# Chunk attention and a hypermixer token MLP on one core: units of 512 tokens by four heads, loads held in line by GpSimd, stores on two queues

## The chip, the core and the metric

The kernel runs on one NeuronCore of a Trainium2 chip. Its engines have a queue of instructions each: PE (TensorE, matmuls; its weight loads are PEld), DVE (VectorE), ACT (ScalarE), POOL (GpSimd) and SP (SyncE, which here only issues DMAs). An engine runs its own queue in order and waits for the others by semaphores. Sixteen DMA engines move data between HBM and the on-chip memory SBUF; matmuls write into PSUM, which has eight banks of 2 KB per partition. The metric is the time of one execution in microseconds on the device, the median of several; all durations below are microseconds.

## The reference

```python
# q, k, v: (8, 8, 576, 64) float32: batch, heads, tokens, head_dim
q_c, k_c, v_c = (x.reshape(B, H, 9, 64, D) for x in (q, k, v))   # chunks of 64 tokens
scores = np.matmul(q_c, k_c.transpose(0, 1, 2, 4, 3)) / np.sqrt(D)
scores = scores - np.max(scores, axis=-1, keepdims=True)
attn = np.exp(scores)
attn = attn / (np.sum(attn, axis=-1, keepdims=True) + 1e-09)
x = np.matmul(attn, v_c).reshape(B, H, S, D).transpose(0, 2, 1, 3).reshape(B, S, H * D)
wq, wk = x @ w_q, x @ w_k                    # w_q, w_k: (512, 64)
W_tok = np.einsum('bsd,btd->bst', wq, wk) / np.sqrt(64)
mixed = np.einsum('bst,btd->bsd', W_tok, x)
out = np.maximum(mixed, 0.0) @ w_out         # w_out: (512, 512); out: (8, 576, 512) float32
```

Attention stays inside chunks of 64 tokens, nine to a batch. The mixing that follows has no softmax, so the kernel forms G = wk^T x (64 x 512) once per batch and then wq G for each token.

## The kernel before, in words

**Units.** Of the nine chunks of a batch, eight make two whole units of 256 tokens by all eight heads (16 units in all); the ninth chunks of two batches make one rest unit (4). `pairs` lists the 20. A whole unit goes through these steps, each named as below and, by its line, in the profile:

- tq and tk (L365): 16 PE transposes each of q and of k into one PSUM bank. Copies (helper `copy`, L287) bring them to SBUF: k in one piece (`kt`, 128x512), q in two halves of 64 partitions into `qbd`, a block-diagonal tile whose other places hold zeros.
- S (L389): 16 matmuls of 128x64, scores of two heads at a time through the block-diagonal q.
- mx and sub on DVE (L402, L412), exp on ACT (L422), E (L434): 8 transposes of the exponentials, and a copy `et`.
- V twice (L464): 16 quarter matmuls each (64x64 of the array, 65 columns, the last a column of ones for the sum), then den, rec and x on DVE (L477, L481, L491).
- xT (L511) and its copy `xt`; pj (L521), both projections in one; `wt`; wkT (L538) and `wk`.

When all of a batch has come so far: G (L575) and its copies `g`, then for each unit mix (L616), relu `rm` (ACT L631 or DVE L629), out (L643) by 512-column matmuls, and the copy into an `osb` tile. Rest units do the same at half the width (tqr, L349).

**What sets the order.** Nothing is scheduled by rule. The table `ORDER` is a list of words such as `6P0`: step 6, on PE, into PSUM bank 0 (V is DVE, S is ACT). `w7` and `n7` are fillers, matmuls on a tile of ones (L675), 512 and 128 columns wide, 9 and 43 of them. `Graph.write` emits the words one after the other, so each engine's queue has them in that order. Buffers come in rings whose depths stand in `RINGS`; a ring that is full makes the next writer wait.

**Loads.** `LOADS` is the order of the loads, all issued by POOL (`load_qk` L204, `load_v` L212, `load_rest` L219), except the first q and k (`wide`), which SP loads as f32 and DVE and ACT cast. A load of q or k of a unit reads 128 rows x 8 heads in pieces of 512 B (two tokens, R = 2), one of v pieces of 256 B, and casts to f16 on the way. There are seven homes for q and k and a ring of ten units (20 tiles) for v. A load is put in POOL's queue once the step that last read its home stands in the order.

```python
def load_qk(u, t):
    nc.gpsimd.dma_start(qk[u][:, t], rows_of((q, k)[t], u))
```

**Stores.** 56 stores, all on SP: 16 of 128 rows (`i == 0`) and 40 of 64. They are held back until the gate, a one-element DMA (L231) that SP waits with for load 76 (counted from 0), the last; then SP issues those held so far (L234), and afterwards each as its `osb` is ready (L226).

```python
def open_gate(of):
    nc.sync.dma_start(gate[:], of)
    st["open"] = True
    for to, x in held:
        nc.sync.dma_start(to, x)
```

Of the kernel before, what the change touches and what calls it, by code (L numbers as in the profile page):

```python
# [20 lines left out]
5V 4V 0S 1S w7 w7 w7 w7 n7 n7 n7 n7 n7 n7 n7 n7 n7 n7 n7 n7 6P0 2V 3S 7V w7 n7 n7 n7 n7 n7 n7 n7 n7  # L21
9P1 8S n7 n7 34P2 10S 35S 11P0 31P2 12V 32S 13V 33S w7 w7 n7 n7 n7 n7 n7 n7 n7 n7 56P3 36P4 58S 14S
59V 37V n7 n7 n7 91P2 57S 15P0 92S 60P3 38V 94P1 93S 95S 61V 39S w7 n7 n7 n7 n7 n7 96P4 62V 116P1
16S 97V 40P3 63S 21P6 41S 64P0 98V 118S 17P2 65S 18V 22V 99S 66P4 23V 19V 24V 117S 67V 20V 100P0
42P6 68V 46P2 69V 25P1 43V 47V 70P4 44V 26S 45V 101S 48V 71S 49V w5 n5 n5 n5 n5 n5 119P1 102P4 120S
106P2 50P0 107V 108V 27P1 109V 51S 72P6 28S 103V 52P0 73S 74P1 29P6 121P2 53S 75V 54P0 30V 163P1
122V 55S 76P0 164S 160P6 77V 104V 78S 105V 79P0 123V 80S 110P7 85P4 124S 83P0 86V 111S 125P1 84S
81P4 126V 161S 162S 127P0 131P2 112P5 128V 132V 129V 133V 89P6 130V 113S 82S 134V 165P0 90S 114P4
135P2 166V 87P3 136S 137P2 167V 88S 138S 210P5 139P2 295P3 115V 140S 211V 168S 141P0 212V 185P1 213V
142S 298V 214P2 143S 169P4 186S 215V 144P6 170V 188P0 145S 216V 150P4 189S 187V 175P6 146P2 296S  # L30
176V 217S 297V 177V 190P0 178V 147S 380P3 151S 191V 218P2 245P6 219V 247S 299P4 192V 248P5 246S
148P2 249S 300V 193S 152P0 301V 149S 382V 220P6 171P4 153S 194P1 221V 172V 173V 383S 154P2 222V 195S
223V 381S 174V 200P0 155S 196P6 224P3 201V 156P4 202V 197V 225S 203V 179P2 226P3 198V 180S 199V
250P0 302S 181P2 157V 204P6 251V 182S 303P4 205S 158P2 304S 227S 252V 183P5 384P4 184S 206P3 159S
228P5 330P6 207S 229V 208P0 332V 273P1 209S 253S 230P0 385V 358P2 331S 231V 270P3 274V 232S 271S
386V 233P0 359S 272V 305P6 333P4 234S 306V 307V 275P2 308V 334S 239P0 276V 237P5 240S 254P4 277V
238S 335P0 255S 241P5 336V 278S 355P2 242S 256P6 337V 279P3 357S 309P4 280S 243P5 257V 258V 356S
259V 281P0 310S 285P2 244S 260P6 282V 235P4 283V 286V 338S 261V 284V 311P5 262V 287V 360P0 263V 312S
236S 339P5 288V 387S 264P6 361V 289P2 265S 388P3 313P4 290S 266P6 362V 291P2 267S 340S 268P6 415P7
389S 314V 269S 292S 390P0 345P4 293P2 391V 418P3 346V 294S 347V 363S 392V 348V 315P2 443P6 393V 316S  # L40
341P4 419S 394P0 342V 364P1 317S 343V 395V 416S 318P2 344V 396P0 365S 417V 324P4 349P1 325V 350S
444S 397V 366P4 319S 370P0 440P6 367V 368V 371V 509P7 372V 441S 373V 420P2 369V 442S 320P0 421V 511S
351P1 510S 374P4 352V 321S 445P6 422V 375S 326P1 446V 376P0 423S 322P2 327S 377V 424P3 447V 398P0
353P1 378P4 399S 484P5 354S 487P0 379V 323S 425V 400P1 448S 488V 430P2 426P6 485S 328P4 431V 432V
427V 433V 486S 449P0 428V 329V 402S 489P2 401S 429V 403P4 490V 434P1 404S 409P6 450S 491V 556P4 410S
# [17 lines left out]
v19a k15 k14 v12a q14 v11a v11b v12b v19b q15 v18a q17 q18 v14b k18 k17 v15b v17b k16 v17a q19 v15a  # L63
v18b v16a k19 v16b
# [643 lines left out]
```

## Time and profile before

| | us |
|---|---|
| median of 3 runs | 141.2 |
| the runs | 138.96, 141.2, 141.28 |
| profiled execution, span | 138.2 |
| PE busy | 121.3 (88%) |
| DVE busy | 107.2 (78%) |
| ACT busy | 99.9 (72%) |
| POOL busy (loads' issues, mostly) | 70.3 (51%) |
| gate, SP waits for it | 92.7, until 95.5 |
| last matmul ends | 130.84 |

The profiled execution is one of its own beside the three timed ones; the page gives its span, 138.2, and no other time for it. In the rows below, `out<-in` are names of tiles, `x16` counts instructions, `| 15.5, 578 |` is the busy time of a group in us and the mean of one in ns, and what follows is the idle time just before them and what ended it. PEclk is the clock granted to PE, 1.00 being full.

### The profile page before, as it was taken

What the parts mean: (1) busy time and instruction counts of PE and PEld (TensorE: products, weight loads), DVE (VectorE), ACT (ScalarE), POOL (GpSimd) and SP (SyncE); (2) the same over time, 40 slices, a digit from 0 to 9 for tenths busy, and PEclk for the clock granted to TensorE, in tenths of its full rate; (3) what the DMA queues carried; (4) which work ended last, traced back from release to release, by engine and by line L of the source; (5) the groups of instructions that cost most, each with busy time, mean ns of one, the idle gap of its engine ahead of it and who ended that gap; (6) DMA issues with size and microseconds to landing.
All of it is one profiled execution on the core that took longest, in us unless ns stands there. A gap on an engine that the chain in (4) does not pass through costs nothing.

```text
span 138.2 us, 5123 instructions
## 1 busy us (share of the span) xinstructions
PE 121.3 (88%) x2184; PEld 88.0 (64%) x2184; DVE 107.2 (78%) x212; ACT 99.9 (72%) x186; POOL 70.3 (51%) x93
## 2 busy tenths in 40 slices
PE   5839996998999999999999949998999999999800
PEld 2627784785578757777677838677785866645300
DVE  6443699879698999999998969999999989644200
ACT  3333699656868988889998939697999886468400
POOL 8999999965658479587959867200000000000000
PEclk9975799999999999999999999999999999999995
DMA  3999999999999999999999999992788596888895
GB/s 113 228 162 178 164 158 162 187 180 137 143 165 175 150 163 183 174 166 168 173 165 167 177 173 170 165 142 22 197 249 254 155 312 196 283 267 181 235 283 143
DMA packets 86185, 25.11 MB, mean 182 GB/s; under 512 B 78994, under 2 KB 81554, under 8 KB 86162
## 3 DMA queue, kind: packets, MB, share of 16 engines
q0 software_dynamic: 78544, 14.29, 140.4%
q1 hardware_dynamic: 7618, 10.49, 26.3%
q8 instruction: 17, 0.28, 0.8%
q14 instruction: 6, 0.05, 0.1%
HBM read 29.62 MB, written 9.44 MB: 283 GB/s over the span
## 4 chain that ended last, share of the span: by engine, by line
PE 67%; ACT 15%; DVE 5%; DMA 5%; issue 3%; SPq 1%; ACTq 0%
PE ps L643 20%; PE ps L365 9%; PE ps L521 6%; PE ps L389 5%; PE ps L616 5%; PE ps L511 5%; PE ps L434 5%; DMA osb<-in_k_dram 5%; PE ps L464 5%; ACT es L422 4%; PE ps L575 3%; ACT qbd L287 3%; ACT et L287 2%; DVE sh L412 2%; PE ps L675 2%
## 5 line engine op out<-in xcount | busy, mean ns | idle before, releaser
L643 PE MATMUL ps<-wo,rm 128*128 128x512 f16 x144 | 36.2, 379 | 0.3 <-ACT rm L631 0.2
L212 POOL DMA_DIRECT2D v_all<-in_v_dram x32 | 28.4, 894 | 7.9 <-DMA v_all<-in_v_dram 2.0
L402 DVE TENSOR_REDUCE mx<-ps 128x16 f32<-128x1024 f32 (+1 forms) x20 | 22.2, 1111 | 4.6 <-PE ps L389 4.1
L491 DVE TENSOR_TENSOR xs<-ps,rec 128x512 f16<-128x512 f32 x36 | 24.1, 686 | 0.5
L365 PE MATMUL ps<-ident,qk 128*64 128x128 f16 x512 | 21.3, 230 | 3.2 <-DVE qk L287 1.6
L365 PEld LDWEIGHTS <-qk 128*64 128x64 f16 x512 | 16.8, 115 | 6.3 <-ACT qk L287 1.8
L422 ACT ACTIVATE es<-sh 128x1024 f16<-128x1024 f32 (+1 forms) x20 | 19.5, 977 | 1.4 <-DVE sh L412 1.1
L643 PEld LDWEIGHTS <-rm 128*128 128x128 f16 x144 | 12.5, 98 | 11.6 <-ACT rm L631 0.8
L412 DVE TENSOR_TENSOR sh<-ps,mx 128x1024 f32<-128x1024 f32 x16 | 19.6, 1222 | 0.3
L287 ACT COPY osb<-ps 128x512 f32<-128x512 f32 x29 | 16.7, 587 | 3.5 <-PE ps L643 3.3
L287 ACT COPY qbd<-ps 64x512 f32<-64x512 f32 (+1 forms) x31 | 16.9, 551 | 3.3 <-PE ps L365 1.9
L631 ACT ACTIVATE rm<-ps 128x1024 f16<-128x1024 f32 (+1 forms) x14 | 13.9, 996 | 3.4 <-PE ps L616 3.2
L204 POOL DMA_DIRECT2D qk<-in_k_dram x15 | 13.5, 902 | 4.4 <-DMA wo<-in_moe_w_out_dram 1.8
L204 POOL DMA_DIRECT2D qk<-in_q_dram x15 | 13.4, 896 | 2.8 <-DMA qk<-in_q_dram 0.9
L287 ACT COPY xt<-ps 128x512 f32<-128x512 f32 (+1 forms) x16 | 8.7, 547 | 5.4 <-PE ps L511 5.1
L616 PE MATMUL ps<-wt,g 128*128 128x256 f16 (+1 forms) x96 | 11.2, 246 | 1.6 <-issue 1.0
L389 PE MATMUL ps<-kt,qbd 128*128 128x64 f16 x288 | 12.1, 196 | 0.1
L389 PEld LDWEIGHTS <-qbd 128*128 128x128 f16 x288 | 10.6, 100 | 1.7 <-issue 0.5
L464 PEld LDWEIGHTS <-et 64*64 64x64 f16 x576 | 7.5, 107 | 6.1 <-issue 2.3
L511 PE MATMUL ps<-ident,xs 128*128 128x128 f16 x144 | 11.1, 219 | 0.0
L521 PE MATMUL ps<-xt,wqk 128*128 128x256 f16 (+1 forms) x80 | 10.8, 261 | 0.0
L434 PE MATMUL ps<-order,es 128*128 128x128 f16 x128 | 9.8, 219 | 1.0 <-ACT es L422 1.0
(59 smaller groups left out, 176.6 us busy)
## 6 DMA issues: line engine op xcount, KB each, us to landing
out_dram<-osb SPq DMA_DIRECT2D x40, 128.0 KB, 2.6
v_all<-in_v_dram POOLq DMA_DIRECT2D x32, 128.0 KB, 8.5
out_dram<-osb SPq DMA_DIRECT2D x16, 256.0 KB, 2.6
qk<-in_k_dram POOLq DMA_DIRECT2D x15, 256.0 KB, 8.9
qk<-in_q_dram POOLq DMA_DIRECT2D x15, 256.0 KB, 8.9
osb<-in_q_dram SPq DMA_DIRECT2D x2, 256.0 KB, 3.1
osb<-in_k_dram SPq DMA_DIRECT2D x2, 256.0 KB, 5.9
wo<-in_moe_w_out_dram POOLq DMA_DIRECT2D x1, 512.0 KB, 8.7
```

The source lines that it names most:

```text
L204: nc.gpsimd.dma_start(qk[u][:, t], rows_of((q, k)[t], u))
L212: nc.gpsimd.dma_start(v_home(u, i)[:, :, 0:D], of)
L287: (nc.vector.tensor_copy if eng == DVE else nc.scalar.copy)(to, of)
L365: nc.tensor.transpose(tp[half(o), j, :, r, :], of, ident[:])
L389: nc.tensor.matmul(sp[:, i, j, c, :], lhsT=st["qb", u][:, j, x].rearrange("p o s -> p (o s)"), rhs=st["kt", u][:, j, x * C : x * C + C], s ...
L402: nc.vector.tensor_reduce(mx[:], scores(), axis=AX.X, op=ALU.max)
L412: nc.vector.tensor_tensor(out=sh[:].rearrange("p x (g r) -> p x r g", r=R), in0=in_banks(bs, 512).rearrange("p i (x r g) -> p (i x) r g", ...
L422: nc.scalar.activation(es[:].rearrange("p x s -> p (x s)"), st["sh", u][:].rearrange("p x s -> p (x s)"), AF.Exp, scale=scale_attn,)
L491: nc.vector.tensor_tensor(out=to, in0=xp()[:, :, :, 0:D], in1=by, op=ALU.mult)
L521: nc.tensor.matmul(pj, lhsT=wqk[:, f].rearrange("p i j -> p (i j)"), rhs=st["xt", u][:, f, :], start=(f == 0), stop=(f == NF - 1),)
L616: nc.tensor.matmul(ma[:, o, f, s], lhsT=st["g", bb][:, (2 * o + f) * P : (2 * o + f) * P + P], rhs=st["wt", u][:, s], start=True, stop=True,)
L643: nc.tensor.matmul(in_banks(bo, DM)[:, 0], lhsT=rm[:, f, i * P : i * P + P], rhs=wo[:, f, :], start=(f == 0), stop=(f == NF - 1),)
```

## The change

**Units.** A unit is now a batch's eight whole chunks, 512 tokens, by four of the eight heads (`(b, w)`, w the half of the heads); the ninth chunks of four batches make one rest unit (numbers 8 and 9). 18 units of one size, taken in the order of `TOKENS`. q and k are read in pieces of 1 KB (four tokens, R = 4).

- T: 32 transposes, k first and then q, into two banks, and one copy of 128x1024 (`qkT`, 17 on ACT and one on DVE). `qbd` and its zeros are gone.
- S: 32 quarter matmuls, 64 columns each, straight from `qkT`.
- The rest of the attention is as before, with two V of 16 quarters. pj and mix use 512 columns; per batch there is one pj, one wkT, one G.
- Each load has its own place for v: `v_all` holds all 36 tiles, so no load of v waits for a V. q and k have four homes of a batch each.

**Loads.** They come by batch. Ahead of most of them POOL runs a `look`: it copies one element of an earlier load into `peek`, and so waits until that one has landed. Which one is set by `INLINE` and `rates`: the latest one after which the loads add up to more than 7.0 at these rates. 56 looks stand in POOL's queue.

**Stores.** The gate is at load 60 (v71); two more loads, v72 and v73, stand behind it. 40 stores, 32 of 128 rows and 8 of 64. From the last load on, `send` shares them out between SP and POOL: 20 each.

**Fillers.** 55, all of 512 columns: 21 ahead of the first T, 34 after it and ahead of batch 2's.

In the diff, `...` marks what is left out.

```diff
-5V 4V 0S 1S w7 w7 w7 w7 n7 n7 n7 n7 n7 n7 n7 n7 n7 n7 n7 n7 6P0 2V 3S 7V w7 n7 n7 n7 n7 n7 n7 n7 n7
...
+4V 0S 1S 2V 3V w0 w0 w0 w0 w0 w0 w0 w0 w0 w0 w0 w0 w0 w0 w0 w0 w0 w0 w0 w0 w0 5P0 6S w2 w2 w2 23P2
+7P0 24S 8V w4 w4 w4 25P2 26V 9V 27V 10S w4 w4 w4 w4 w4 w4 w4 w4 w4 w4 w4 w4 11P4 28S 12V w5 w5 29P5
...
-k1 q1 rk0b rq0b rk0a rq0a q3 k3 q4 v0a v0b rv0b v1a rv0a v1b k4 v3a v3b wq wk k5 q5 wo v4b v4a rk1b
-rq1b rq1a rk1a q6 k6 v5b v5a q8 k8 rv1a rv1b v6a v6b q11 k9 q9 k12 k11 v8a v14a q16 v9a q12 v9b v8b
...
+k0b q0b v00 wq wk v01 v02 v03 rk0a rk0b rq0a rq0b rv0a rv0b k1 q1 wo v10 v11 v12 v13 k2 q2 v20 v21
+v22 v23 k3 q3 v30 v31 v32 v33 rk1a rk1b rq1a rq1b rv1a rv1b k4 q4 v40 v41 v42 v43 k5 q5 v50 v51 v52
+v53 k6 q6 v60 v61 v62 v63 k7 q7 v70 v71 v72 v73
 """
-GATE = 76
+GATE = 60
...
+INLINE = 7.0
...
+    TOKENS = [0, 8, 1, 2, 3, 9, 4, 5, 6, 7]
...
     RINGS = {
-        "qb": 3, "kt4": 3, "kt2": 2, "mx2": 3, "mx1": 2, "sh2": 2, "sh1": 1, "es2": 2, "es1": 1,
-        "et2": 2, "et1": 1, "xs2": 8, "xs1": 4, "xt2": 2, "xt1": 1, "wt2": 8, "wt1": 4, "wk": 8,
-        "wkr": 4, "rm2": 4, "rm1": 1, "g16": 5, "den": 4, "rec": 4, "osb": 24,
+        "qkT": 3, "mx": 3, "sh": 2, "es": 2, "et": 2, "xs": 6, "xt": 4, "wt": 3, "wk": 3, "rm": 3,
+        "g16": 5, "den1": 3, "rec1": 3, "den2": 3, "rec2": 3, "rmr": 2, "osb": 23, "osb2": 1,
     }
...
-    qbd = [const.tile([P, HP, 4, 2, C], F16, name=f"qbd{n}") for n in range(RINGS["qb"])]
...
-    v_all = const.tile([P, 2 * NV, H, VW], F16, name="v_all")
+    v_all = const.tile([P, B * NT + 4, H, VW], F16, name="v_all")
...
+    def rows_of(x, b):
+        return x[b, :, 0:TOK, :].rearrange("h (p r) d -> p h (r d)", r=R)
+
...
-    def v_home(u, i):
-        return v_all[:, 2 * (whole.index(u) % NV) + i]
...
+    def load_qk(t, b, part):
+        nc.gpsimd.dma_start(qk[b][:, t, hs(part)], rows_of((q, k)[t], b)[:, hs(part)])
+
+    def load_v(b, m, part):
+        of = v[b, hs(part), P * m : P * m + P, :].rearrange("h p d -> p h d")
+        nc.gpsimd.dma_start(v_all[:, NT * b + m, hs(part), 0:D], of)
+
...
+    held, count = [], {"sp": 0, "pool": 0}
+
+    def send(to, of):
+        if st.get("last") and count["pool"] < count["sp"]:
+            count["pool"] += 1
+            nc.gpsimd.dma_start(to, of)
+        else:
+            count["sp"] += 1
+            nc.sync.dma_start(to, of)
 
     def store(to, of):
-
         if "open" in st:
-            nc.sync.dma_start(to, of)
+            send(to, of)
         else:
             held.append((to, of))
 
...
+    def look(of):
+
+        nc.gpsimd.tensor_copy(peek[0:1, :], of)
...
+    line = []
     for n_load, key in enumerate(LOADS.split()):
-        if n_load == 8:
...
+        rates = {256: 14.5, 512: 22.9, 1024: 39.7, 2048: 73.0}
+        line.append((n * rates[size] / 16000, last))
+        seen = next((m for m in range(n_load, -1, -1) if sum(x for x, _ in line[m:]) > INLINE), -1)
+        if 0 <= seen < n_load and INLINE:
+            graph.queue.append((lambda of=line[seen][1]: look(of()), lambda: []))
+        graph.queue.append((emit, lambda after=after: [s for bw in after for s in turned[bw]]))
...
+    graph.queue.append((lambda: st.__setitem__("last", True), lambda: []))
...
-        def evs(bk, t, of, n1):
-            def ev_q(eng, o):
-                to = qb[half(o), :, 0:nx, o, :].bitcast(F32)
-                copy(eng, to, of()[half(o)].rearrange("p j (x s) -> p j x s", x=nx))
-
-            def ev_k(eng):
-                tt = ring([P, HP, nx * C], F16, f"kt{nx}")
-                copy(eng, tt[:].rearrange("p j s -> p (j s)").bitcast(F32), of().rearrange("p j s -> p (j s)"))
-                st["kt", u] = tt
...
+            def pe_t(eng):
+                tp = in_banks(bt, 512, F16).rearrange("p t (j c r g) -> p t j c r g", j=2, c=8, r=R)
+                for t in (1, 0):
+                    for j in range(2):
+                        for n in range(4):
+                            for o in range(2):
+                                if rest < 0:
+                                    of = qk[b][:, t, HQ * w + 2 * j + o, n * D : n * D + D]
+                                    to = tp[half(o), t, j, :, n, :]
...
+                                nc.tensor.transpose(to, of, ident[:])
...
+        def ev_t(eng):
+            tt = ring([P, 2, 2, 2, 4, C], F16, "qkT")
+            to = tt[:].rearrange("p b j a y s -> p b (j a y s)").bitcast(F32)
+            copy(eng, to, in_banks(bt, 512))
+            st["qkT", u] = tt
...
-            sp = in_banks(bs, 512).rearrange("p i (j c s) -> p i j c s", j=HP, c=2)
-            for i in range(ni):
-                for j in range(HP):
-                    for c in range(2):
-                        x = 2 * i + c
+            sp = in_banks(bs, 512).rearrange("p o (j y s) -> p o j y s", j=2, y=4)
+            for j in range(2):
+                for y in range(4):
+                    for o, a in QUARTERS:
                         nc.tensor.matmul(
-                            sp[:, i, j, c, :],
-                            lhsT=st["qb", u][:, j, x].rearrange("p o s -> p (o s)"),
-                            rhs=st["kt", u][:, j, x * C : x * C + C],
+                            sp[half(a), o, j, y, :],
+                            lhsT=turned_at(0, o, a, j, y),
+                            rhs=turned_at(1, o, a, j, y),
                             start=True,
                             stop=True,
                         )
 
...
+            def pe(eng, o=o, bm=bm):
+                for f in range(MIX):
+                    nc.tensor.matmul(
+                        in_banks(bm, TOK)[:, f].rearrange("p (a i s) -> p a i s", a=2, i=NT),
+                        lhsT=st["g", b][:, (MIX * o + f) * P : (MIX * o + f) * P + P],
+                        rhs=st["wt", b][:].rearrange("p i a s -> p a i s"),
+                        start=True,
+                        stop=True,
+                    )
```

The first place is POOL's queue where batch 5's k and q are loaded. `qk_82` to `qk_88` before, and `qk_76` to `qk_79` now, are the homes of q and k; the bracket has the semaphores of DMA queues and engines that a row waits for. Before:

```order
L204 DMA qk_83<-in_q_dram 128x8x128 [waits DMASW7_49,PE_49]
L204 DMA qk_82<-in_k_dram 128x8x128 [waits DMASW0_49,DVE_49,Activation_49]
L204 DMA qk_82<-in_q_dram 128x8x128 [waits DMASW1_49]
L204 DMA qk_84<-in_k_dram 128x8x128 [waits DMASW2_49,PE_49]
L204 DMA qk_83<-in_k_dram 128x8x128 [waits DMASW3_49]
L212 DMA v_all<-in_v_dram 128x8x64 [waits DMASW4_49]
```

The loads follow each other, each waiting for the load eight before it. Now, in the same queue:

```order
L254 COPY peek<-qk_76 1x1 [waits DMASW4_49,Pool_49]
L211 DMA qk_77<-in_k_dram 128x8x256 [waits DMASW1_49,PE_49]
L254 COPY peek<-v_all 1x1 [waits DMASW6_49,Pool_49]
L211 DMA qk_77<-in_q_dram 128x8x256 [waits PE_49]
L254 COPY peek<-v_all 1x1 [waits DMASW7_49,Pool_49]
L215 DMA v_all<-in_v_dram 128x8x64
```

A look now stands ahead of each load, and waits for a load that is less far back.

The second place is PE's queue at the transposes that read the second load into a home: `qk_84` before, and now `qk_77`, home of batches 1 and 5 (T:5.1). Before:

```order
L643 LDWEIGHTS rm_1580
L643 MATMUL ps<-wo,rm_1580 128x512
L365 LDWEIGHTS qk_84 [waits DMASW0_49]
L365 MATMUL ps<-ident,qk_84 64x4x32 [waits DVE_49]
L365 LDWEIGHTS qk_84
L365 MATMUL ps<-ident,qk_84 64x4x32
```

And now:

```order
L489 LDWEIGHTS et
L489 MATMUL ps<-v_all,et 64x65
L368 LDWEIGHTS qk_77 [waits DMASW1_49]
L368 MATMUL ps<-ident,qk_77 64x8x16 [waits DVE_49]
L368 LDWEIGHTS qk_77
L368 MATMUL ps<-ident,qk_77 64x8x16
```

In both, PE stands at the first transpose until the load has landed; now a load brings eight heads of 512 tokens, and a V stands ahead of it instead of an out.

The third place is the end of SP's queue, the last stores; the numbers tell `osb` tiles apart. Before:

```order
L226 DMA out_0_dram<-osb_3099 128x512
L226 DMA out_0_dram<-osb_3106 128x512
L226 DMA out_0_dram<-osb_3113 64x512 x2
L226 DMA out_0_dram<-osb_3121 64x512 x2
L226 DMA out_0_dram<-osb_3129 64x512 x2
L226 DMA out_0_dram<-osb_3133 128x512
```

Now:

```order
L238 DMA out_0_dram<-osb_3187 64x512
L238 DMA out_0_dram<-osb_3207 128x512
L238 DMA out_0_dram<-osb_3231 128x512
L238 DMA out_0_dram<-osb_3258 64x512
L238 DMA out_0_dram<-osb_3266 128x512
L238 DMA out_0_dram<-osb_3280 128x512
```

And on POOL, behind all loads:

```order
L235 DMA out_0_dram<-osb_3220 128x512
L235 DMA out_0_dram<-osb_3251 128x512
L235 DMA out_0_dram<-osb_3258 64x512
L235 DMA out_0_dram<-osb_3273 128x512
L235 DMA out_0_dram<-osb_3283 128x512
```

The stores of a tile's two halves were two in a row on SP; most tiles now go out in one, every second one on POOL, the very last (`osb_3283`) among these.

More of the change, by code (lines that the diff above doesn't have):

```diff
@@ new lines @@
+            last = lambda i="qk".index(key[1]): wqk[0:1, NF - 1, i, 0:1]
+        graph.loads.append((key, "POOL", n, size))
+        rates = {256: 14.5, 512: 22.9, 1024: 39.7, 2048: 73.0}
[4 more added lines that the diff above has]
+        graph.queue.append((emit, lambda after=after: [s for bw in after for s in turned[bw]]))
@@ L674, in idle @@
+    done = set()
+    for b in TOKENS:
+        for w in range(2 if b < REST else 1):
+            attention(b, w)
+        project(b)
+        done.add(b)
+        for z in WHOLE:
+            if ("g", z) not in st and z in done and REST + z // 4 in done:
+                mixing(z)
     def idle(i, cols):
```

729 lines of the change are left out of this document (367 added, 362 removed).

## The prediction

> **What bounds the kernel now.** The page comes first: the share of busy time, the chain that ended last, the queues.
>
> ```profile
> PE 121.3 (88%) x2184; PEld 88.0 (64%) x2184; DVE 107.2 (78%) x212; ACT 99.9 (72%) x186; POOL 70.3 (51%) x93
> ...
> q0 software_dynamic: 78544, 14.29, 140.4%
> ...
> HBM read 29.62 MB, written 9.44 MB: 283 GB/s over the span
> ...
> PE 67%; ACT 15%; DVE 5%; DMA 5%; issue 3%; SPq 1%; ACTq 0%
> ...
> out_dram<-osb SPq DMA_DIRECT2D x40, 128.0 KB, 2.6
> ...
> qk<-in_k_dram POOLq DMA_DIRECT2D x15, 256.0 KB, 8.9
> ```
>
> PE leads, but 88% is an average over stretches with different limits. The chain, in order of time, gives the pitch of each PE step where nothing interrupts it (start, duration, engine, line):
>
> ```profile
> 2.35 6.58 DMA osb<-in_k_dram
> ...
> 9.62 0.64 PE ps L365 x6
> ...
> 41.92 0.67 PE ps L575 x10
> ...
> 101.39 0.38 PE ps L464 x32
> 101.77 1.01 PE ps L365 x32
> ...
> 105.40 0.67 PE ps L575 x10
> ...
> 107.85 0.47 PE ps L389 x16
> ...
> 108.76 0.45 PE ps L434 x8
> 109.64 0.45 PE ps L511 x8
> ...
> 120.62 0.12 PE ps L538 x4
> ...
> 126.51 4.33 PE ps L643 x20
> 130.86 0.58 ACT osb L287
> ```
>
> The first load is under way from about 2 and lands at 8.9; first transposes at 9.62; the matmuls end at 130.84 (126.51 + 4.33). At these pitches the matmuls of the whole kernel come to 103.0: tq and tk 32 x 0.505 with four tqr of 0.45 (eight of 128 columns, as the E row) is 18.0, S 8.5, E 8.1, V 36 x 0.19 = 6.8, xT 8.1, G 8 x 0.67 = 5.4, out 36 x 0.866 (a 512-column matmul is 4.33 / 20 = 0.2165) = 31.2, the two projections and mixing 17.0. Between the ends of the two G steps above (42.6 and 106.1) stand, counted step by step along PE's order, 55.9 of those 103.0, so 7.6 of 63.5 are lost; after 106.07 stand 24.4 in 24.8, so nothing is. What differs is DVE (columns: stretch, length, then PE, PEld, DVE, ACT, POOL busy with counts, clock, DMA, GB/s):
>
> ```profile
> 42.60:106.10 63.50, 60.86 (x1275) 46.19 (x1273) 59.32 (x118) 55.22 (x107) 34.11 (x39) 1.00 1.84 170
> 106.07:130.84 24.77, 24.76 (x308) 15.27 (x308) 17.04 (x35) 17.20 (x32) 0.00 (x0) 1.00 0.81 231
> ```
>
> In the first stretch DVE is busy 93%, 0.503 each for 118 instructions, and ACT 87%: PE loses 7.6 waiting for evacuations. In the second DVE is at 69% and PE waits for nobody. The end is another matter; SyncE's own rows:
>
> ```profile
> 95.53 0.74 SPq L231 DMA_DIRECT2D gate<-v_all  x1
> 96.31 9.36 SPq L234 DMA_DIRECT2D out_dram<-osb  x14
> 105.77 29.45 SPq L226 DMA_DIRECT2D out_dram<-osb  x42
> ...
> 134.68 0.54 SPq L226 DMA_DIRECT2D out_dram<-osb  x1
> ```
>
> The gate opens when the loads are over, at 95.5; then 56 stores stand in one queue at 0.70 each (29.45 / 42), back to back. The last is issued 3.2 after the last copy (130.86 + 0.58 = 131.4), lands 2.6 after its issue (137.3), and 0.9 closes the span at 138.2. So three limits lie near each other: the loads until 95.5, the evacuations in the middle, the store queue at the end.
>
> **The change, part by part.** *PE work.* T is the same transposes by the same pitch (18 x 1.01 = 18.2 against 18.0). S becomes 32 quarter matmuls of 64 columns; the nearest row is V's, 32 quarters of 65 columns in 0.38, so 18 x 0.38 = 6.8 against 8.5. If a quarter cost as much as a whole matmul of S (0.47 / 16), S would be 18 x 0.94 = 16.9; below 0.38 nothing speaks for. I take 0.38, the same shape. Projection and mixing move the same columns. Sum 101.3, so -1.7. Fillers: 55 of 512 columns at 0.2165 are 11.9; before, 9 such and 43 of 128 columns (0.45 / 8) are 4.4. Of the 55, 21 stand before the first transposes, under the first load, and 34 (7.4) between T:0.0 and batch 2's first, T:2.1.
>
> *Evacuations.* The copies of transposed q and k:
>
> ```profile
> L287 ACT COPY qbd<-ps 64x512 f32<-64x512 f32 x27 | 15.5, 578 | 2.2 <-PE ps L365 1.9
> ...
> L631 ACT ACTIVATE rm<-ps 128x1024 f16<-128x1024 f32 x13 | 13.3, 1027 | 3.4 <-PE ps L616 3.2
> ...
> L287 ACT COPY kt<-ps 128x512 f32<-128x512 f32 x13 | 7.6, 586 | 1.3 <-PE ps L365 1.1
> ...
> L629 DVE TENSOR_SCALAR rm<-ps 128x1024 f16<-128x1024 f32 x3 | 3.7, 1225 | 1.9 <-PE ps L616 1.8
> ...
> L287 DVE COPY qbd<-ps 64x512 f32<-64x512 f32 x5 | 3.4, 688 | 0.2
> ...
> L287 DVE COPY kt<-ps 128x512 f32<-128x512 f32 x3 | 2.0, 676 | 0.0
> ```
>
> For the whole units these four groups of qbd and kt are 28.5. After, one 128x1024 copy for each of 18 units: 17 on ACT at the 1.027 of rm (same shape) and one on DVE at 1.225, 18.7. Some 10 leave, mostly ACT's, and a little more with the rest units.
>
> *Loads.* The cost of one packet is 16 engines x bytes landed / GB/s, in stretches with one kind of packet (f32 is read and half as many bytes of f16 land: q0's 14.29 MB of the 29.62 read):
>
> ```profile
> 16.00:18.00 2.00, 1.66 (x44) 1.40 (x41) 1.72 (x3) 1.95 (x4) 2.00 (x3) 1.00 2.41 155
> 26.00:28.00 2.00, 1.92 (x62) 1.60 (x60) 1.51 (x5) 1.51 (x4) 2.00 (x4) 1.00 1.48 198
> 46.00:48.00 2.00, 2.00 (x41) 1.59 (x40) 1.87 (x6) 1.88 (x4) 0.69 (x1) 1.00 3.08 144
> 52.00:55.00 3.00, 3.00 (x71) 2.26 (x69) 2.86 (x12) 2.48 (x7) 2.67 (x4) 1.00 1.83 183
> ```
>
> The rows at 16 and 46 are v pieces of 256 B read: 16 x 128 / 155 = 13.2 and 14.2 ns, say 14. The row at 52 is 512 B q and k: 16 x 256 / 183 = 22.4. The row at 26 mixes 512 B with wo's 2 KB pieces: 198 GB/s over 2.0 is 396 KB; with 543 pieces of 512 B counted in it (139 KB landed, 0.76 of its 2.0) 251 pieces of 2 KB take the other 1.24, 79 ns. A 1 KB piece was not read before: the straight line between 22.4 and 79 gives 41, doubling the 512 B piece 45; I take 42, near the line, since the row at 26 shows larger pieces moving more bytes. Two 512 B pieces become one: 3 ns of 45 saved, some 6% of the q and k time. The order matters more. PE is in order, and its last wait for a load that can matter is the q half of batch 5 at T:5.1 (by the sum below, q6 and q7 are there at 76.5 and 85.5, and T:6.1 and T:7.1 are reached near 82 and 89). Ahead of that load come 12,288 pieces of 1 KB, 33,792 of 256 B (v of batches 0 to 4, both rest sets, the small weights) and wo: (12,288 x 42 + 33,792 x 14 + 512 x 79) / 16 = 32.3 + 29.6 + 2.5 = 64.4; with 2.0 before the stream starts and 1.0 to land, q5 is there at 67.5. The same way batch 2 is there at 35.2, batch 4 at 58.5, the last load near 89, so the gate opens some 6 earlier.
>
> Without any wait PE would reach T:5.1 at 9.6 + 40.5 + 7.4 = 57.5 (40.5 is the work ahead of it by the pitches, 7.4 the fillers). So load waits of up to 10 hide the fillers, the start-up and hand-offs of that part; if the loads were early, the 7.4 would be paid in full.
>
> *The looks.* Ahead of most loads POOL reads one element of a load 7 older by the planner's rates, 56 times; the rows of a load's issue and, nearest to the reading, of a small POOL instruction:
>
> ```profile
> L212 POOL DMA_DIRECT2D v_all<-in_v_dram x32 | 28.4, 894 | 7.9 <-DMA v_all<-in_v_dram 2.0 <-DMA qk<-in_k_dram 1.9 <-DMA qk<-in_q_dram 1.8
> ...
> L692 POOL MEMSET const-uint8-127<- 128x1 uint8 x1 | 0.1, 111 | 0.0
> ```
>
> 56 x 0.11 = 6.2 beside 67 issues of 0.894 = 60 fits into 87. What waits behind a look is only POOL's own next loads. If 7 in flight feed the queues as the 8.9 from issue to landing do now, it is free; I take free, and keep the other end as a rival.
>
> *After q5.* PE has left half of T:5.1 and all behind it: T 6.5 x 1.01, S 7 x 0.38, E 8 x 0.45, V 17 x 0.19, xT 10 x 0.45, G 5 x 0.67, out 29 x 0.866, projection and mixing 11.3, together 60.3, of which 44.4 to the last V. Beside those 44.4 stand 80 DVE instructions, by 0.503 each 40.2 busy, at 93% 43.1. Before it was 59.32 beside 55.9, DVE over PE; now PE is the longer by a little. Lost time is between 0 (as after 106.07) and 6.0 (7.6 / 55.9 of 44.4); I take 2.0, since the sign of the difference has turned but barely. PE ends at 67.5 + 60.3 + 2.0 = 129.8.
>
> *The end.* 40 stores instead of 56, half on SP (20 x 0.70) and half on POOL, have 40 to leave in: no backlog, 3.2 saved. The last store is POOL's. Its landing has a low bound of 2.6 (SP's) and a high one of 5.5, a small load among others on POOL's queue:
>
> ```profile
> wqk<-in_moe_w_q_dram POOLq DMA_DIRECT2D x1, 64.0 KB, 5.5
> ```
>
> With the queues empty by then I take 3.7, nearer the first. [...] Tail: 0.6 + 3.7 + 0.9 = 5.2. Span 135.0, 3.2 less than 138.2. The median of the runs shown is 141.2, 3.0 above the span; kept as it is, 138.0.
>
> **The rivals.** *Loads come early (F).* If the stream does better than my sum, so that the middle is paced by batch 2 and by PE: 35.2 + 87.4 of work behind that load + 4.7 lost (5%) = 127.3, span 132.5, 135.5. For it: the 198 GB/s row leaves room for a 1 KB piece below 42 ns, and each 3 ns less bring q5 2.3 forward. Against: the same sum done for the loads of before ends at 91.8, 3.7 short of the real 95.5, so it tends to promise loads too early, not too late. 0.18.
>
> *A 1 KB piece costs by the byte (Y).* At 45 ns q5 comes 12,288 x 3 / 16 = 2.3 later: 140.3. For it: the row at 52 has 512 B pieces at 2 x 183 = 366 GB/s read, and that may be near a ceiling. Against: the row at 26, with 2 x 198. 0.13. [...]
>
> *Hand-offs lose as before (H).* The order by table is tight; if 13.6% is lost in the 44.4, that is 6.0 instead of 2.0, at 142.0; the place is a two-bank copy on ACT, which gives its banks back after 1.03 instead of 0.58 and now stands whole between T and S. Against: some 10 less of copies. 0.19.
>
> *The line of looks starves the queue (L), slower.* Place: POOL, from the first look on. With 7 in flight where landing takes 8.9, the rate would fall to 7 / 8.9 and q5 come at 67.5 / 0.79 = 85; with half of that effect at 76.2, PE ends at 138.5 and the time is 146.7. It decides from q5 at 73.5 (144.0), a rate 9% down. Against it: the row at 52 moves 183 GB/s with less under way on the engines (DMA 1.83) than the row at 46 has for its 144 (3.08), so more in flight is not what makes the rate. 0.13.
>
> **How the numbers follow.** The forecast has 0.37, between 135.5 and 140.5 on its own (lost time 0 to 4, landing 2.6 to 5.5, not all at one end). Faster by over 2% means under 138.4, slower over 144.0; 2% of 141.2 is 2.8, about what a measurement of this kernel can tell from none. Faster: 0.18 of F, 0.22 of the forecast, 0.03 of Y and H with luck at the end: 0.43. Slower: 0.11 of L, 0.05 of H together with Y (144.3), 0.03 for S at more than 0.38 a unit: 0.19. Same: 0.38. The range takes F with nothing lost (130.8, so 131.5) up to H with Y: 131.5 to 145.0; L at half effect and beyond, and F with more than that, are left out.
>
> **What would show it.** Right: T:5.1 is PE's last long wait on a load, near 67; the gate at 89; S at 0.38 for 32; qkT on ACT near 1.03; the last POOL issue within 1 of the last copy. Wrong: looks that wait while the rate falls under 160 GB/s (L); q5 before 63 (F); PE waits on qkT or on DVE above 4 after T:5.1 (H); S rows of 0.47 or more; a landing of the last store above 5.5.

## The result: 155.1 against 140.8, and where the time went

The changed kernel takes 155.1 (154.5 to 155.9), the kernel before 140.8 (138.96 to 141.28): a ratio of 1.108, with a 95% interval of 1.098 to 1.118. Ratios, here and below, are of the executions in the chip's fast state alone, so they can differ a little from the ratio of the medians. The forecast was 138.0, with a range of 131.5 to 145.0. The profiled execution of the changed kernel took 154.5, with a span of 152.8.

Its page, the lines that answer to those of before:

```profile
PE 127.4 (83%) x2435; PEld 79.3 (52%) x2435; DVE 99.0 (65%) x183; ACT 90.9 (60%) x134; POOL 78.9 (52%) x157
...
q0 software_dynamic: 64496, 19.01, 113.0%
...
DMA 33%; issue 32%; POOL 19%; PE 12%; ACT 1%; POOLq 1%
...
v_all<-in_v_dram POOLq DMA_DIRECT2D x32, 128.0 KB, 6.3
...
qk<-in_k_dram POOLq DMA_DIRECT2D x7, 512.0 KB, 6.1
qk<-in_q_dram POOLq DMA_DIRECT2D x7, 512.0 KB, 8.0
```

The chain was PE's (67%); now it is made of loads, POOL and "issue". The chain in order of time, and the waits by engine (total, times, longest):

```profile
18.41 6.94 DMA qk<-in_k_dram
...
46.46 8.14 DMA qk<-in_q_dram
...
74.29 7.64 DMA qk<-in_q_dram
...
81.97 0.64 PE ps L368 x16
...
93.57 0.38 PE ps L400 x32
...
94.11 1.50 issue
```

```profile
ACT qkT L321 <- PE ps L368: 22.2, 11, 5.6
DVE mx L411 <- PE ps L400: 19.7, 8, 7.5
POOL peek L254 <- DMA qk<-in_k_dram: 13.6, 7, 4.7
...
PE ps L368 <- DMA qk<-in_q_dram: 10.1, 5, 2.8
```

The q half of batch 5 is there at 81.97, not at 67.5. PE waits five times, 10.1 in all, for q at T (T:1.1 to T:5.1); ACT and DVE, no longer the tight ones, wait for PE. Why the loads are late stands in POOL's timeline, around the looks (start, duration, and in brackets the idle time before and what ended it):

```profile
18.41 0.88 POOL L211 DMA_DIRECT2D qk<-in_k_dram  x1
19.40 0.18 POOL L254 COPY peek<-qkr 1x1 f16<-1x1 f16 x1
19.86 0.88 POOL L211 DMA_DIRECT2D qk<-in_q_dram  x1 [0.27 <-issue]
25.47 0.18 POOL L254 COPY peek<-qk 1x1 f16<-1x1 f16 x1 [4.73 <-DMA qk<-in_k_dram]
25.92 0.75 POOL L299 DMA_DIRECT2D wo<-in_moe_w_out_dram  x1 [0.28 <-issue]
```

```profile
22.00:26.00 4.00, 3.56 (x65) 1.89 (x56) 3.24 (x4) 1.65 (x3) 0.26 (x2) 1.00 1.29 174
26.00:28.00 2.00, 0.03 (x2) 0.00 (x0) 0.00 (x0) 0.52 (x1) 2.00 (x5) 1.00 0.80 106
```

After k and q of batch 1 POOL stands at a look until k has landed, 4.73. Then only what is left of q is in flight, and the next load, issued at 25.92, has nothing moving yet: in the stretch 26 to 28 the rate falls from 174 to 106 GB/s. The gate opens at 104.3 instead of 95.5.

The sum of the forecast, term by term: q5 at 82.0 instead of 67.5 (+14.5); 60.3 of PE work behind it, in which 5.2 were lost instead of 2.0 (+3.2; the matmuls end at 143.85 + 3.62 = 147.5); tail 5.3 instead of 5.2:

```profile
104.26 0.74 SPq L247 DMA_DIRECT2D gate<-v_all  x1
105.05 42.54 SPq L238 DMA_DIRECT2D out_dram<-osb  x20
```

```profile
143.85 3.62 PE L701 MATMUL ps<-wo,rm 128*128 128x512 f16 x16
```

So the rival L is what happened, and q5 is not far from its full price (85). That nearness is partly chance: without the looks q5 is 3.8 late all the same, as the first experiment shows. The experiments ask what else is in the 14.

### The profile page after: what moved, and what is told of

It reads as the page before. It is cut to its first block, busy times and chain, and to the rows that moved or that the text cites. A ratio compares the mean times of both kernels' runs of the same rounds, so it can differ in the third digit from the quotient of the medians.

```text
span 152.8 us, 5612 instructions
## 1 busy us (share of the span) xinstructions
PE 127.4 (83%) x2435; PEld 79.3 (52%) x2435; DVE 99.0 (65%) x183; ACT 90.9 (60%) x134; POOL 78.9 (52%) x157
## 4 chain that ended last, share of the span: by engine, by line
DMA 33%; issue 32%; POOL 19%; PE 12%; ACT 1%; POOLq 1%
DMA qk<-in_q_dram 10%; DMA v_all<-in_v_dram 9%; DMA qk<-in_k_dram 9%; POOL out_dram L235 5%; DMA wo<-in_moe_w_out_dram 5%; PE ps L701 4%; POOL v_all L224 3%; PE ps L368 2%; POOL peek L254 2%; POOL qkr L219 2%; POOL qk L211 2%; POOL v_all L215 2%; POOL g L271 2%; PE ps L671 1%; PE ps L536 1%
## 5 line engine op out<-in xcount | busy, mean ns | idle before, releaser
L411 DVE TENSOR_REDUCE mx<-ps 128x16 f32<-128x1024 f32 x18 | 21.9, 1222 | 21.0 <-PE ps L400 19.7
L321 ACT COPY qkT<-ps 128x1024 f32<-128x1024 f32 x17 | 17.2, 1012 | 22.2 <-PE ps L368 22.2
L368 PE MATMUL ps<-ident,qk 128*64 128x128 f16 x512 | 19.7, 231 | 12.2 <-DMA qk<-in_q_dram 10.1
L235 POOL DMA_DIRECT2D out_dram<-osb x20 | 11.0, 549 | 36.6 <-ACT osb L321 32.0
L368 PEld LDWEIGHTS <-qk 128*64 128x64 f16 x512 | 16.6, 116 | 16.0 <-DMA qk<-in_q_dram 10.9
L427 ACT ACTIVATE es<-sh 128x1024 f16<-128x1024 f32 x18 | 19.1, 1059 | 6.6 <-DVE sh L421 5.8
L755 PE MATMUL ps<-ones 128*128 128x512 f16 x55 | 15.4, 420 | 1.5 <-DVE ones L185 1.5
L660 ACT ACTIVATE rm<-ps 128x1024 f16<-128x1024 f32 x12 | 12.2, 1025 | 0.5 <-PE ps L671 0.4
L440 PEld LDWEIGHTS <-es 128*128 128x128 f16 x144 | 8.9, 100 | 6.5 <-ACT es L427 4.8
L321 ACT COPY xt<-ps 128x512 f32<-128x512 f32 x14 | 8.2, 588 | 6.4 <-PE ps L536 6.3
L536 PEld LDWEIGHTS <-xs 128*128 128x128 f16 x128 | 8.0, 100 | 3.7 <-issue 2.1
L400 PEld LDWEIGHTS <-qkT 64*64 64x64 f16 x576 | 6.6, 114 | 6.1 <-issue 3.4
```

Of the source, the lines that this page charges most:

```text
L235: nc.gpsimd.dma_start(to, of)
L321: (nc.vector.tensor_copy if eng == DVE else nc.scalar.copy)(to, of)
L368: nc.tensor.transpose(to, of, ident[:])
L411: nc.vector.tensor_reduce(mx[:], of, axis=AX.X, op=ALU.max)
L427: nc.scalar.activation(to, st["sh", u][:].rearrange("p x s -> p (x s)"), AF.Exp, scale=scale_attn)
L440: nc.tensor.transpose(ep[:, n], of, (order if rest < 0 else ident)[:])
```

## The experiments

Each compares with runs of the kernel before on the same chip (medians of 140.2 to 141.2); times are medians, and a ratio, with its interval in brackets, is to the kernel before. Changed kernels ran on several chips, so a difference of 1 to 2 between two of them is weak evidence.

### The looks, and the stores shared out

**No looks.** `-INLINE = 7.0` `+INLINE = 0` in the changed kernel.

> The changed kernel without its 56 looks, all else as it is. Line theory (the looks, with POOL's own issue time behind each, leave the DMA queues empty): POOL runs ahead again, q of batch 5 lands at 70 to 74 instead of 81.9, the gate opens near 95 instead of 104.3, and the time falls from 155 to 143 to 147. Piece theory (a 1 KB piece simply costs more than 42 ns): q5 stays above 78 and the time within 3 of 155. Hand-off theory (the order itself loses the time): q5 comes early, as in the first, but the time stays above 150.

148.6, ratio 1.058 (1.048 to 1.069): 6.5 less than with looks. q5 landed at 71.3, and the last load at 92.6. A window with nothing but 1 KB pieces:

```profile
66.00:68.00 2.00, 2.00 (x82) 1.60 (x77) 0.85 (x1) 2.00 (x5) 1.67 (x2) 1.00 1.45 197
```

16 x 512 / 197 = 41.6 ns a piece: the 42 of the forecast holds when the queue is fed, so the piece theory falls. But the time is above the 143 to 147 of the line theory: no T waits for its load any more except by 0.1, and still PE reaches T:5.1 only at 76.4 and ends at 142.3. Something else is in it.

**Looks 14 behind.** `-INLINE = 7.0` `+INLINE = 14.0`.

> The changed kernel with looks that stay 14 instead of 7 behind. Line theory by depth (7 in flight is too few): within 2 of the kernel without looks. Line theory by POOL time (a look and the pause around it delay POOL's next issue, however far back it looks): little better than 155, at most 4 less. Piece theory: no change from 155.

148.4, 1.056 (1.046 to 1.067), as without looks. It was the depth, 7, that cost 6.5, and not POOL's time for a look.

**The looks in the kernel before**, 7 behind, with the same rates:

```diff
+        rates = {256: 14.5, 512: 22.9, 1024: 39.7, 2048: 73.0}
+        line.append((n * rates[size] / 16000, last))
+        seen = next((m for m in range(n_load, -1, -1) if sum(x for x, _ in line[m:]) > INLINE), -1)
+        if 0 <= seen < n_load and INLINE:
+            graph.queue.append((lambda of=line[seen][1]: look(of()), lambda: []))
```

> The kernel before with the same looks, 7 behind, ahead of its own loads, all else as it was. Line theory: its loads end 8 to 12 later than 95.5 and the time rises from 141 to 148 to 153. Piece and hand-off theories: within 2 of 141.

146.4, 1.043 (1.034 to 1.052): 5.4 more, a little under the line theory's 148. Its loads end at 102.2, 6.7 later than the 95.5 of before and not quite the 8 to 12 expected. The looks alone cost about as much in either kernel.

**The stores of the kernel before on SP and POOL by turns**, by the changed kernel's `send`.

```diff
-            nc.sync.dma_start(to, of)
+            send(to, of)
```

> The kernel before with its 56 stores shared out one by one between SP and POOL from the gate on, all else as it was. If SP's queue of 56 issues at 0.70 sets its end, as the forecast had it: the last issue comes within 1 of the last copy instead of 3.2 after it, 2 to 3 less than 141. If the end is PE's alone: within 1 of 141.

141.0, 1.001 (0.995 to 1.007): no change. The last issue came 0.3 after the last copy (132.9 against 132.6), so the line at SP is gone, but in that execution the matmuls ended 1.1 later than in the profile of before.

### Fillers, and the place of wo

**Without the 34 fillers behind the first transposes, looks kept:** the 34 words `w…` behind `5P0` are taken out of `ORDER`.

> The changed kernel with its looks, without the 34 fillers that stand behind the first transposes. If the waits for late loads hide them, as the forecast had it (T:1.1 to T:5.1 wait 11 in all there): within 2 of 155. If they are paid: 5 to 7 less, 148 to 150.

154.7, 1.087 (1.075 to 1.098): within 1 of 155.1. q5 lands at 82.1, as with the fillers (81.9). Late loads do hide them.

**Without those fillers and without looks.**

> Neither looks nor those 34 fillers. Without looks no T waits for its load any more, so by the path theory the 7.4 of fillers are paid in full and go: 141 to 143 against 148.6. By the hidden theory another load takes their place (v13 at V:1.1, landing 34.5; q2 landing 39.4, now 1.7 ahead of its T): at most 3 less, 145.5 to 148.6.

149.3, 1.056 (1.047 to 1.065), no better than 148.6. What takes their place is the wait at T:1.1 (2.0, for q1), 3.9 at an E for ACT's exp, and a lower clock (0.5 to 0.8 in five of the slices 5 to 11 of 40). Taking the 7.4 out gains nothing even now; the path theory falls.

**wo behind v13, no looks:** `-k1 q1 wo v10 v11 v12 v13 k2` `+k1 q1 v10 v11 v12 v13 wo k2` in `LOADS`.

> No looks, and wo loaded behind v13 instead of ahead of v10. V:1.1 waits 3.4 there for v13, which now lands 2.5 earlier. If that wait is on the path: 146 to 147 against 148.6. If later waits take it up: within 1 of 148.6.

147.0, 1.039 (1.030 to 1.048): 1.7 less. PE's longest wait at V:1.1 (line 489) fell from 3.4 to 1.5, here without and with wo moved (total, times, longest):

```profile
PE ps L489 <- issue: 3.9, 2, 3.4
```

```profile
PE ps L489 <- issue: 2.5, 2, 1.5
```

But v13 is not shown to be the cause. With wo moved it lands at 30.47, before PE gets there at 30.73, and PE still waits 1.5. Both waits stand at a boundary between two blocks of 256 of PE's instructions, and end 1.3 to 1.5 after a 16 KB transfer of the instruction queue has landed, as the section on PE's instructions shows. With wo in its old place v13 (34.46) and the transfer (33.04 and 1.48 more) both fit PE's going on at 34.52. The two profiled executions are also 1.4 apart at the third step T already (21.05 and 19.61), ahead of what the moved load can change. What made the 1.7 is open.

**Both: no fillers, wo moved, no looks.**

> No looks, no fillers behind the first transposes, wo behind v13. If fillers and the wait for v13 each hold the path: 139 to 142, beside the kernel before or under it. If PE's hand-offs and what it waits for next set the pace: 144 to 147.

149.0 (147.1 to 150.3) against 147.0 (146.0 to 148.2) with the fillers: no gain, and far from 139 to 142. The page's row of granted clock, in 40 slices, of this kernel and of the one with the fillers:

```profile
PEclk9999659559999999999999999999999999999998
```

```profile
PEclk9999999999999999999999999999999999999999
```

Without fillers the clock falls to 0.5 to 0.6 in slices 5, 6, 8 and 9 (14.7 to 33); with them it stays at 0.9 or more. So the fillers may pay for themselves in clock; that this is why nothing is gained was not tested apart.

### PE's instructions

The kernel with wo moved (147.0) has its last load at 91.9 (95.5 before) and, fillers aside, no more PE work by the pitches than before, and is 6 slower. The view of waits for PE, in the stretch 36 to 92, has these rows of "issue" from 1.0 up, in this kernel and in the one before:

```profile
PE ps L536 <- issue: 2.2, 1, 2.2
PE ps L630 <- issue: 1.5, 1, 1.5
PE ps L400 <- issue: 1.5, 1, 1.5
PE ps L489 <- issue: 1.1, 1, 1.1
```

```profile
PE ps L616 <- issue: 1.0, 1, 1.0
```

"issue" is a wait for nothing that the view knows, at four different lines. Counted along PE's queue (matmuls and weight loads), all five come at the same place: at instruction 193 or 194 of a block of 256. The records of the instruction queue (q8, transfers of 16 KB) fit it. Worked out from the records: the boundary's number, when PE reached the boundary before it, start and landing of the last q8 transfer, when PE passed this boundary, and the longest idle time there.

```
no looks
  961   27.23   32.00   33.04   34.52   3.38
wo moved, no looks
  961   25.91   30.14   31.08   32.38   1.55
 1217   32.38   36.14   37.08   38.57   1.30
 1473   38.57   42.61   43.59   45.04   1.97
 1729   45.04   49.14   50.13   51.49   0.64
 2497   62.98   66.10   66.99   68.49   1.58
 3265   81.71   85.18   86.11   87.62   2.36
before
 1985   54.50   58.72   59.67   61.18   0.25
 2241   61.18   65.16   66.10   67.67   0.00
 2753   74.77   78.21   79.19   80.62   1.37
```

With wo moved a transfer starts 2.2 to 4.3 (3.6 on average) after PE passed the last boundary, for the boundaries from 25 to 88, while loads run. Where they are over it is 2.5 after the boundary at 94.2, when the held stores go out, and 0.9 and 0.6 after those at 99.8 and 105.4. It takes 0.9 to 1.1, and where PE stalls it goes on 1.3 to 1.5 after the landing: some 6.4 for 256 instructions. The trace of before has, from 42 to 94, 5.9 to 7.1 from boundary to boundary and little idle time there (2.3 in the whole execution); the kernel without looks has 10.9, the one with wo moved 10.3. The changed kernel as it stands, with looks, has only 3.1: after five of its boundaries from 25 to 84 the transfer starts within 0.0 to 0.9, at places where the looks let the stream of loads run low: 60 to 141 GB/s in the microsecond behind four of them (182 behind the fifth, at 25.7, and 106 from 26 to 28), against 168 to 188 over the four waits of 2.5 to 3.8 from 40 to 80 in the same trace. So the looks cover a part of this cost, which shows when they are gone.

The changed kernel has 4,885 PE instructions against 4,391, since S is 32 quarter matmuls, each with its weight load, where it was 16. The pages have 19 transfers of the instruction queue for the changed kernel and 17 for the one before (transfers, MB, share of 16 engines):

```profile
q8 instruction: 19, 0.31, 0.8%
```

```profile
q8 instruction: 17, 0.28, 0.8%
```

One transfer of 16 KB for every 256 PE instructions fits both (4,885 / 256 = 19.1, 4,391 / 256 = 17.2). That each brings PE its next block is read from these counts and the times above, not tested. The theory that follows from it, called the fetch theory below, is that PE gets its blocks no faster than at the pace above, some 6.4 for 256, while loads run; the work theory is that only PE's own time counts.

**Small matmuls put into the kernel before, and as much PE time in large ones.** Ahead of eight steps S in `ORDER`:

```diff
+            for n in range(16):
+                for a in range(2):
+                    to, of = ps[half(a), i, 32 * n : 32 * n + 32], ones[half(a), 0:64]
+                    nc.tensor.matmul(to, lhsT=of, rhs=of[:, 0:32], start=True, stop=True)
```

and, in the other kernel, one or two words `w` of 512 columns at the same places.

> The kernel before with 8 groups of 32 small matmuls (64x64 of the array, 32 columns, two at a time) on the tile of ones, put ahead of eight steps S between 46 and 86: 512 PE instructions more (4,881, about as many as the changed kernel's), at most 3.0 of PE time. Fetch theory (PE cannot get its blocks of 256 instructions faster than one in 6.2 to 6.5 while the loads run): two more blocks, 7 to 13 more, 148 to 154. Work theory (only PE's time counts): at most 3 more, 141 to 144.

> The same eight places, but 14 fillers of 512 columns in all, 28 PE instructions and the same 3.0 of PE time. Fetch theory and work theory alike: 0 to 3.5 more, 141 to 144.5, and under the kernel with the small matmuls by 5 or more if the fetch theory holds.

150.4, 1.080 (1.070 to 1.090), with the small ones; 140.8, 1.011 (0.997 to 1.025), with the large ones. The small ones cost 9.6 more than the large ones. Not all of that is theirs. In the profiled executions the kernel with the small ones is 3.8 behind the other already ahead of the first small matmul, where both queues are still the same: two of the rest units' loads landed late, and PE waited 2.5 for them (L349 below), with a clock of 0.6 in the slice of the page behind it. Why they came late is not shown, and whether they did so in the other executions is not known. The rows of its waits, 36 to 92, from 1.0 up (L679 are the small matmuls):

```profile
PE ps L679 <- issue: 3.3, 3, 1.4
PE ps L349 <- DMA qkr<-in_k_dram: 1.4, 1, 1.4
PE ps L365 <- issue: 1.2, 2, 0.9
PE ps L349 <- DMA qkr<-in_q_dram: 1.1, 1, 1.1
```

Counted from the first group on, against the profile of before, the 512 small instructions cost 9.1 and the 28 large ones 3.0, their own time. An undisturbed group takes 0.61, not the 0.38 assumed, so the small ones' own time is 4.9, and 4.2 is beyond it: about what the idle time at the block boundaries grew by (4.1). The work theory falls, by 4.2 and not by the whole 9.6. The same stretch of both, small first:

```profile
42.00:96.00 54.00, 47.66 (x1098) 37.14 (x1099) 40.55 (x84) 37.95 (x73) 35.94 (x41) 0.97 2.11 164
```

```profile
42.00:96.00 54.00, 50.43 (x1007) 37.84 (x1003) 47.99 (x96) 43.12 (x84) 34.04 (x39) 1.00 2.06 160
```

In 54 PE ran 2,197 and 2,010 instructions, 40.7 and 37.2 a microsecond, and 448 of the 2,197 are the small ones put in, so DVE and ACT got 84 and 73 of their instructions done instead of 96 and 84.

**Looks 10 behind, wo moved.** `+INLINE = 10.0`.

> The changed kernel with wo behind v13 and looks that stay 10 behind, between 7 (which starves) and none. If a queue of loads that is less deep lets the blocks of instructions through sooner: fetches start 2.5 to 3.2 after their block boundary instead of 3.6, stalls at the boundaries 5 to 8 instead of 10, time 143.5 to 146 against 147.0 without looks. If 10 starves too: 149 or more. If depth does not matter here: 146 to 148.

149.1, 1.071 (1.056 to 1.086): 2 more than without looks. The transfers of instructions started 3.6 after the boundaries on average, as without; the last load came 2 later (94.0), and T:1.1 waited 1.3 for its k and 2.0 for its q. Idle time at the boundaries fell to 6.7, inside the 5 to 8 expected, but not because the transfers came sooner: PE reached some boundaries later. A depth of 10 gained nothing, and it did not let the instructions through sooner; only at 7, where the stream runs low, some came sooner, as said above.

**Fewer fillers in the kernel before:** its 43 of 128 columns become 13 of 512, `-n7 n7 n7 n7` `+w7`.

> The kernel before with its 43 fillers of 128 columns put together into 13 of 512, 60 PE instructions less at about the same PE time. Fetch theory: every later block boundary comes 60 instructions further along, 0.5 to 1.5 less, 139.5 to 140.5. Work theory: within 0.7 of 141.

140.95, 1.012 (1.000 to 1.024): no change clear of noise, so the 0.5 to 1.5 less of the fetch theory did not show. These 60 instructions stand ahead of 30 us. There, in the profile of before, the transfers landed at 14.45, 23.65 and 29.99, and PE passed the boundaries 5.8, 2.6 and 1.7 later.

**S with half as many instructions, in the changed kernel without looks and with wo moved.** S makes other products than the reference's, as the expectation says.

```diff
-                    for o, a in QUARTERS:
+                    for o in range(2):
                         nc.tensor.matmul(
-                            sp[half(a), o, j, y, :],
-                            lhsT=turned_at(0, o, a, j, y),
-                            rhs=turned_at(1, o, a, j, y),
+                            in_banks(bs, 512)[half(o), j, 128 * y : 128 * y + 128],
+                            lhsT=turned_at(0, o, 0, j, y),
+                            rhs=st["qkT", u][half(o), 1, j, :, y, :],
```

> The changed kernel without looks and with wo behind v13, and S by 16 matmuls of 128 columns instead of 32 of 64: as many columns, half the instructions (576 less on PE, 4,309 in all). It leaves out the scores of every second chunk and has products of two different chunks in their place; every other step and wait stays. Fetch theory: 2.25 blocks of 256 less to be fetched under the loads, stalls at the block boundaries 2 to 5 instead of 10, time 138 to 142.5 against 147.0. Work theory (S costs its columns): 146.5 to 148.

142.5, 1.024 (1.012 to 1.036): 4.5 less than 147.0 for 576 instructions, with the same columns; measured from the kernel before on each chip, 3.7 less (2.3 above it instead of 6.0). S itself is slower in this form, 0.57 a unit instead of 0.38, 3.4 more in all, so the gain is not in S's own time. Idle time at the block boundaries is 1.7 in place of 10.3, and in the stretch 36 to 92 "issue" is down to one row:

```profile
PE ps L400 <- issue: 0.5, 1, 0.5
```

**The rest units' transposes two heads at a time:** `-for o in range(2):` `+for o in range(2 if rest < 0 else 1):`, 64 instructions less.

> The changed kernel without looks, wo behind v13, and the two rest units' transposes done for two heads at a time: 64 PE instructions less, the output unchanged. Fetch theory: a quarter of a block, 0.5 to 1.6 less, 145.4 to 146.5. Work theory: within 0.7 of 147.0.

148.9 with a spread of 146.0 to 149.8: unclear, neither theory's number.

**The gate of the kernel before four loads earlier.** `-GATE = 76` `+GATE = 72`.

> The kernel before with its gate at load 72 instead of 76, so that SP begins its stores some 4 earlier, beside the last four loads. If SP's queue sets the end: the last issue comes within 1 of the last copy instead of 3.2 behind, 1 to 2.5 less, 138.5 to 140. If the stores slow the last loads as much as they gain, or PE's end moves: within 1 of 141.

140.0, 1.001 (0.995 to 1.006): no change. The stores began at 91.9 instead of 96.3; the last was issued 2.2 after the last copy instead of 3.2, but the matmuls ended at 132.4 instead of 130.8.

No version here beats the kernel before.

## Why the prediction was wrong

**The looks: the step that failed most.** "If 7 in flight feed the queues as the 8.9 from issue to landing do now, it is free; I take free." It is not: 6.5 by the run without them, 5.4 in the kernel before. The landing row itself (8.9) said how much was in flight when the engines were fed, and L's price for q5, 85, came near the 81.97 (of which 3.8 are not the looks'). But L was given 0.13, and the range left it out. The argument against it, more GB/s at a smaller DMA share, compared a row of 512 B pieces with one of 256 B: the share goes with the kind of piece in the rows here (2.41 and 3.08 for 256 B, 1.83 for 512 B, 1.45 for 1 KB), and no row shows that it tells how deep the queue is. The time that counts is from a landing to the first packet of the load issued on it: 25.3 to 27.4 here, while some 1.5 of work was left in flight (581 pieces of 1 KB by the packets' records, at 42 ns).

**S: "I take 0.38, the same shape."** The pitch is right (0.38 for 32 in the row at 93.57), and so is 6.8 for S in all. But a step was costed by PE's time alone, and PE's instructions had a pace of their own while loads ran (some 6.4 for 256 with wo moved, 10.3 of idle time at the boundaries). Where -1.7 was forecast, S's instructions cost 3.7 by the run with half of them, although S's own time is 3.4 more there. V, the row that served as the nearest, is as dense in instructions, but stood in the kernel before between steps with fewer; that this hid its price there is argued, not tested. (The sum of PE work, 101.3, leaves out the 0.2 that T grows by; nothing hangs on it.)

**"PE's last wait for a load that can matter is the q half of batch 5": right** in the kernel as it was forecast, where T:5.1 at 81.97 is the last of the five waits. What failed there is q5's time, and with it the looks. Without looks no T waits, and moving wo behind v13 is 1.7 less; that a wait for v13 was the reason is not shown.

**The 7.6 lost in the middle of the kernel before, put down to evacuations.** The rows of waits do not bear this out. From 42.6 to 106.1 PE's waits in that trace are 2.5 in all, 1.5 of them on DVE and ACT, and the longest (1.0, L616) is a block boundary. Where the rest of the 7.6 goes is open.

**The stream.** The price of a 1 KB piece (42, measured 41.6) and the sum of pieces were right, but not the start. The 1.0 to land in that sum was the author's estimate; in the changed kernel T went on 1.2 after q5's last 1 KB piece had ended, and 0.3 to 0.4 after those of q1 to q4. Without looks q5 came at 71.3, 3.8 late; q of batch 2 came at 39.4 instead of 35.2, q of batch 4 at 62.2 instead of 58.5, the last load at 92.6 instead of 89. So all of the lateness is there by batch 2, and the sum holds behind it. Ahead of it the 256 B pieces of the rest units and of v are issued by POOL one short load after another. The stretch 8 to 20 of the kernel without looks, POOL busy 11.90 of 12:

```profile
8.00:20.00 12.00, 9.33 (x144) 5.17 (x140) 6.18 (x6) 4.07 (x4) 11.90 (x17) 0.86 2.05 139
```

The forecast set POOL's 66 against 87 as a whole, and so did not see that it is full in this stretch. That POOL's issuing holds the loads there is read from this row, not tested.

**The fillers: right** with looks, where late loads hide them (154.7). "If the loads were early, the 7.4 would be paid in full" did not come true: without looks they can be taken out and nothing is gained (149.3), with a lower clock. **Evacuations: right in size** (qkT 1.012 on ACT, 1.217 on DVE, against 1.027 and 1.225); no run shows what they are worth, and ACT and DVE wait for PE here. **The tail: right in length by luck** (5.3 for 5.2). The last store lands 2.6 after the last copy and not 3.7, and the span closes 2.0 after that and not 0.9. The line at SP is gone, as forecast; but neither sharing the stores nor an earlier gate changes the time of the kernel before, so "3.2 saved" was no gain that a run shows there.

**The sum of what is shown,** each kernel against the one before on the same chip: 14.3 above it as changed, 7.6 without looks, 6.0 with wo moved too, 2.3 with half of S's instructions. So looks are 6.6, the place of wo 1.6 (within the spread of these runs, cause open), S's instructions 3.7. What the 2.3 left are is open: the matmuls of that kernel by the pitches, fillers among them and S at its 0.57, are some 9 more than before's, but taking fillers out did not shorten the kernels without looks.

**The rivals.** F and Y fell with q5 and with the 41.6. H had a loss of 6.0 behind q5, and 5.2 came, but not for its reason: behind T:5.1 the view of waits shows none of PE on DVE or ACT, and its two longest, the 1.50 at 94.11 and 0.5 at an S, stand at block boundaries. The rest of the 5.2 is not explained.

## What to carry to other kernels

Before a load is made to wait for an older one, add up what is left in flight when that one lands (here 1.5) and compare it with the time until the new load's first packet (here 2.0): here it was less, and the rate fell from 174 to 106 GB/s. And price a step by its instructions too: where loads run all along, count PE's instructions over the stretch (40.7 and 37.2 a microsecond is what it got here, in two kernels from 42 to 96). Of two forms with the same columns try the one with fewer and larger matmuls: here it won, 142.5 against 147.0, although its own time was 3.4 longer.

## What the runs showed of the hardware

While loads ran, the next 16 KB transfer of the instruction queue started 2.2 to 4.3 after PE had passed a boundary between blocks of 256 instructions (wo moved; 3.4 to 4.2 in the kernel before from 41 to 88) and took 0.9 to 1.1, and where PE stalled at the boundary after it, PE went on 1.3 to 1.5 after the landing. In the changed kernel it started within 0.0 to 0.9 after five boundaries; behind four of them the looks had let the stream of loads run low, to 60 to 141 GB/s. Such a stall was "issue" in the view of waits, at whatever line stood at the boundary: up to 2.4 in the kernel with wo moved. In the kernel before, 512 small matmul and weight-load instructions cost 4.2 more than their own time of 4.9, by the profiles; 28 large ones cost their own time, 3.0.
